# Talking-heads attention and gated network: rows issued ahead of stores, and some loads issued by GpSimd instead of SyncE

## The chip, the cores and the metric

One core of one Trainium2 chip runs the kernel. The metric is the device time of one execution in microseconds, median of several; lower is better. The engines are TensorE (PE, with its weight loads as PEld), VectorE (DVE), ScalarE (ACT), GpSimd (POOL) and SyncE (SP). SP does no arithmetic: it only issues DMAs, in program order, and waits before an issue for what that DMA needs. POOL and ACT can issue DMAs too, each in its own program order.

## The reference

```python
# q, k, v: (4, 12, 448, 64); w_pre, w_post: (12, 12)
scores = q @ k.T / sqrt(64)                                # per batch and head
scores = einsum('bhij,hg->bgij', scores, w_pre)            # heads mixed before the softmax
attn = exp(scores - max) ; attn = attn / (sum + 1e-9)
attn = einsum('bhij,hg->bgij', attn, w_post)               # and after it
out = attn @ v
x = out.transpose(0, 2, 1, 3).reshape(1792, 768)
result = (sigmoid(x @ w_gate) * (x @ w_val)) @ w_out       # 768 -> 1536 -> 768
```

All is float32 on the outside; the gated network's weights come in as 8-byte numbers, of which the kernel makes float32 itself.

## The kernel before

The kernel has two parts that overlap a little: the attention, which ends near 350 us, and the gated network, which runs to the end.

**The attention** goes over four batches, each with four blocks of query rows (three of 120 rows, one of 88). A block's scores are computed head pair by head pair (`scores`, line 159), copied from PSUM into a staging tile `st` (`keep`, line 165), and from there cut into *units* of 20 query rows (six units a block, five in the last block of a batch, 92 in all). For a unit, `regroup` (lines 203, 205) issues two DMAs that move rows of `st` into a tile `T`, so that the heads of a row lie on partitions; there are four T buffers. Then come `premix` (PE, line 213: heads mixed), `rowmax` (DVE, 218), `expo` (ACT, 225), `norm` (POOL 230, then DVE's reciprocal 231), `scale` (POOL, 237: the high half `ph`), `p_lo` (DVE, 243: the low half `pl`), `postmix` (PE, 255), `mix` (ACT, 263), and per block `av` (PE, 282), which ACT copies into a tile `xt` (line 292; one buffer for nearly all blocks). `xt` is put on a list `stores`, and `flush` issues its store to `xs` in DRAM (line 271, on SP).

The loop over *slots* s (line 404) sets the order. In a slot, in program order: `flush()`, the rows for unit s+6 (`rows_until(s + LEAD, ...)`, line 406), norm and scale of unit s+1, premix and rowmax of unit s+3, a score job, the first exp of unit s+3, p_lo of unit s+1, postmix and mix of unit s, the second exp of s+3, then what the plan has for this slot (loads of k, q and v among it), a piece of the gated network's work (`moe.slot`), and last `av` and the steps of `moe.early`. A block's `xt` are written at the ends of two slots two apart, and flushed at the start of the next slot.

The plan (lines 302 to 348) puts loads of a batch's `k` (six, line 137), a block's `q` (line 145) and a batch's `v` (three, line 172) into slots well ahead of their use, and the steps of eight weight tiles of the gated network (`early`, line 1032): four DMAs that load a tile in pieces into `raws` (line 1037), then steps on ACT, DVE and POOL that make float32 of it, and a DMA from POOL that keeps the result (line 1096). Before the change all of these loads are issued by SP, between the rows and the stores. The first batch's loads stand ahead of the loop and name their queue.

**The gated network** (class `_Moe`) multiplies in seven products per pair of tiles, on operands split into two float16 halves; PE's matmuls are on lines 1147 and 1158. A planner written in Python (`order_tasks`) fixes the order of its tasks.

Of the kernel before, what the change touches and what calls it, by code (L numbers as in the profile page):

```python
# [15 lines left out]
I8 = mybir.dt.int8  # L16
# [25 lines left out]
def _attention(ctx, tc, ins, B, H, S, D, xs, raws, make_moe):  # L42

    nc = tc.nc
    qp, kp, vb = (ins[n] for n in ("qp", "kp", "vb"))
    NQ = H // QUAD
    NP = H // 2
# [32 lines left out]
    def qk_banks():  # L80
        return [ps_qk.tile([128, 512], F32, tag="qk", name="qk") for _ in range(2)]
# [52 lines left out]

    def k_load(b, c, eng=None):
        t = kst.tile([128, S], F32, tag="k", name="k")
        (eng or nc.sync).dma_start(out=t, in_=kp[b, c])
        k_t[b, c] = t

    def q_load(bi, eng=None):  # L140

        b, i0, _, _, sets = blocks[bi]
        n = R * sets
        t = qst.tile([128, NP * QB], F32, tag="q", name="q")
        (eng or nc.sync).dma_start(out=t[:, :NP * n], in_=qp[b, :, NP * i0:NP * (i0 + n)])
        if n < 100:
            nc.gpsimd.memset(t[:, NP * n:NP * n + 100 - n], 0.0)
        q_t[bi] = [t[:, c * n:] for c in range(NP)]
# [4 lines left out]
    def scores(bi, c, sc):  # L153
        b, n = blocks[bi][0], R * blocks[bi][4]
        q, k = q_t[bi], k_t[b, c]
        for s0, s1 in ((0, 64), (64, max(n, 100))):
            for e in range(2):
                rows = slice(64 * e, 64 * e + 64)
                nc.tensor.matmul(sc[e][s0:s1, :S], lhsT=q[c][rows, s0:s1], rhs=k[rows, :], start=True, stop=True)  # L159

    def keep(bi, c, e, sc):
        n = R * blocks[bi][4]
        if c == e == 0:
            st_t[bi] = stg[bi % ST].tile([QB, H, S], F32, tag="st", name="st")
        (nc.vector.tensor_copy if e else nc.scalar.copy)(st_t[bi][:n, 2 * c + e], sc[e][:n, :S])  # L165
# [3 lines left out]

    def v_load(b, u):  # L170
        t = vst.tile([128, QUAD, 4, D], F32, tag="v", name="v")
        nc.sync.dma_start(out=t.rearrange("p h j d -> p (h j d)"), in_=vb[b, u])
        vt[b, u] = t


# [21 lines left out]
    def regroup(u):  # L197
        bi, r0s, _, _, i = units[u]
        sets, st, T = blocks[bi][4], st_t[bi], t_bufs[u % len(t_bufs)]
        at = 64 - HK  # L200
        for x in range(2):
            if len(r0s) == 2:
                nc.sync.dma_start(out=T[at:at + 2 * HK, x], in_=st[i + x:sets * R:sets])
            else:
                nc.sync.dma_start(out=T[at:at + HK, x], in_=st[i + sets * HALF * x:sets * HALF * (x + 1):sets])

    def premix(u):
        T = t_bufs[u % len(t_bufs)]
        banks = units[u][2]
        for x in range(2):  # L210
            for i, bank in enumerate(banks):
                rows = slice(64, 64 + HK) if i else slice(0, 64)
                nc.tensor.matmul(pm[bank][64 * x:64 * x + 64, :S], lhsT=w1[rows], rhs=T[rows, x], start=True, stop=True)  # L213

    def rowmax(u):
        nm = sm.tile([128, 2], F32, tag="nm", name="nm")
        for i, bank in enumerate(units[u][2]):
            nc.vector.tensor_reduce(nm[:, i:i + 1], pm[bank][:, :S], axis=AX.X, op=ALU.max, negate=True)  # L218
        nm_t[u] = nm

    def expo(u, i):
        if i == 0:
            e_t[u] = ep.tile([128, 2, S], F32, tag="e", name="e")
            ss_t[u] = sm.tile([128, 2], F32, tag="ss", name="ss")
        nc.scalar.activation(out=e_t[u][:, i], in_=pm[units[u][2][i]][:, :S], func=AF.Exp, bias=nm_t[u][:, i:i + 1],  # L225
                             scale=1.0, accum_out=ss_t[u][:, i:i + 1])

    def norm(u):
        ss = ss_t[u][:, :len(units[u][1])]
        nc.gpsimd.tensor_scalar(ss, ss, 1e-9, 1.0 / P_UP, op0=ALU.add, op1=ALU.mult)  # L230
        nc.vector.reciprocal(ss, ss)  # L231

    def scale(u):

        ph = pp.tile([128, 2, S], F16, tag="ph", name="ph")
        for i in range(len(units[u][1])):
            nc.gpsimd.tensor_scalar(ph[:, i], e_t[u][:, i], ss_t[u][:, i:i + 1], 1.0, op0=ALU.mult, op1=ALU.mult)  # L237
        p_t[u] = [ph]

    def p_lo(u):  # L240
        pl = pp.tile([128, 2, S], F16, tag="pl", name="pl")
        for i in range(len(units[u][1])):
            nc.vector.scalar_tensor_tensor(pl[:, i], e_t[u][:, i], ss_t[u][:, i:i + 1], p_t[u][0][:, i],  # L243
                                           op0=ALU.mult, op1=ALU.subtract)
        p_t[u].append(pl)
# [14 lines left out]
    def mix(u):  # L260
        bi, r0s = units[u][:2]
        out = mixes[bi % 2].rearrange("p j h s -> p (j h) s")[:, :, r0s[0]:r0s[-1] + R]
        nc.scalar.activation(out=out.rearrange("p g (y r) -> p y g r", r=HALF), in_=mx_t.pop(u), func=AF.Copy,  # L263
                             scale=1.0 / (P_UP * W_UP))
# [4 lines left out]
    def flush():  # L269
        while stores:  # L270
            nc.sync.dma_start(out=stores[0][0], in_=stores.pop(0)[1])
# [26 lines left out]
    LEAD = 6  # L298
# [12 lines left out]
    for b in range(B):  # L311
# [3 lines left out]
        s = f + 5  # L315
        for i in range(H // 2):
            s = max(s + 1, f + 6 + 2 * (2 * i // QUAD))
# [51 lines left out]
    for c in range(1, NP):  # L369
        k_load(0, c, nc.sync)  # L370
# [26 lines left out]
    def rows_until(u, done):  # L397
        while done < min(NU, u + 1):
            regroup(done)
            done += 1  # L400
        return done

    next_dma = 0
    for s in range(min(min(plan), -LEAD), max(plan) + 1):
        flush()
        next_dma = rows_until(s + LEAD, next_dma)
        todo = plan.get(s, ())
        jobs = [args for fn, args in todo if fn is scores]
        ahead_u = [(s + SOFT, i) for i in range(len(units[s + SOFT][1]))] if 0 <= s + SOFT < NU else []
        if 0 <= s + 1 < NU:  # L410
            norm(s + 1)
            scale(s + 1)
        if ahead_u:
            premix(s + SOFT)
            rowmax(s + SOFT)

        def job(bi, c):
            sc = qk_banks()
            scores(bi, c, sc)
            return lambda e: keep(bi, c, e, sc)  # L420

        kept = job(*jobs[0]) if jobs else None
        for i, e in enumerate(ahead_u[:1]):
            expo(*e)
        if kept:
            kept(0)
            kept(1)
        for c in hooks.get(s, ()):
            c.close()
        if 0 <= s + 1 < NU:  # L430
            p_lo(s + 1)
        tail = (av, moe.between, moe.early)
        if s == NU - 1:
            nc.scalar.activation(out=iw, in_=sw, func=AF.Sigmoid)
        if 0 <= s < NU:
            postmix(s)
        elif s >= NU:
            moe.slot(NG + s - NU)
        if 0 <= s < NU:
            mix(s)  # L440
        for e in ahead_u[1:]:
            expo(*e)
        for fn, args in todo:
            if fn is not scores and fn not in tail:
                fn(*args)
        if s >= NU - LEAD - 3:
            next_dma = rows_until(s + 1 + LEAD, next_dma)
        if 0 <= s < NU:
            for i in range(len(units[s][1])):
                moe.slot(units[s][3] + i)  # L450
        for fn, args in todo:
            if fn in tail:
                fn(*args)
        for args in jobs[1:]:
            kept = job(*args)
            kept(0)
            kept(1)
# [22 lines left out]
class _Moe:  # L480
# [14 lines left out]
    NP = 7  # L495
# [536 lines left out]
    def early(self, k, step):  # L1032

        raw = self.free["R"][k % len(self.free["R"])]
        if step < 4:
            b, e = 2 * self.WE * step, min(2 * self.WE * (step + 1), 8 * self.WE - 3)
            self.nc.sync.dma_start(out=raw.bitcast(I8)[:, b:e], in_=self.src[k].bitcast(I8)[:, b + 3:e + 3])
            return
        names = ("raw", k), ("half", k)
        self.at.update({names[0]: raw, names[1]: self.free["H"][0]})  # L1040
        if step < 9:
            self.top(k, (0, 0, 1, 2, 2)[step - 4], self.nc.vector if step > 5 else None, (0, 1, None, 0, 1)[step - 4])
        elif step < 11:
            self.convert(names[0], k, step - 9)
        elif step < 13:
            self.sum_of(names[0], ("w", k // 4), k % 4, step - 11, self.at[names[1]].bitcast(F16))
        else:
            self.keep_w(names[0], k)
        for name in names:
            del self.at[name]  # L1050
# [242 lines left out]
```

## Time and profile before

| what | value |
|---|---|
| median of 3 runs (lowest, highest) | 790.5 us (789.5, 790.78) |
| profiled execution: its own time | 792.71 us |
| profiled execution: span from first to last instruction | 790.9 us |
| PE busy | 765.7 us (97%) |
| DVE busy | 631.6 us (80%) |
| ACT busy | 566.5 us (72%) |
| POOL busy | 256.0 us (32%) |
| mean granted clock | 0.995 |
| HBM read, written | 87.77 MB, 38.15 MB |

The busy time of PE is modelled, so that a PE that is "busy" need not be at its peak. "Idle before" is the time in which an engine waited, with what ended the wait; where a wait is for several things, the one that came last by the profile is named, and where the engine named had long been done it was another. The chain that ended last is followed back from the last instruction to whatever released it. DMA issues that SP makes appear in the timeline as SPq; their duration is that of the issue and not of the transfer.

### The profile page before, as it was taken

How to read it: one execution, taken by the hardware profiler on the slowest of the kernel's cores; microseconds unless marked ns; L12 is line 12 of the kernel's file. 1: busy time of each engine (PE TensorE's matmuls, PEld its weight loads, DVE VectorE, ACT ScalarE, POOL GpSimd, SP SyncE). 2: the span in 40 equal slices, each digit the busy share in tenths (PEclk: the TensorE clock that was granted, in tenths of full speed). 3: DMA queues.
4: the chain of work that ended last, by engine and by line, in shares of the span. 5: the costliest groups of instructions: out<-in, count | busy, mean ns of one | idle time of the engine just before them, and what ended most of it. 6: DMA issues, size and time to landing. Idle time of an engine off the chain costs nothing.

```text
span 790.9 us, 23630 instructions
## 1 busy us (share of the span) xinstructions
PE 765.7 (97%) x9626; PEld 422.9 (53%) x9626; DVE 631.6 (80%) x1092; ACT 566.5 (72%) x1122; POOL 256.0 (32%) x426
## 2 busy tenths in 40 slices
PE   8999999899989999978999999999999999999998
PEld 2465665566656666554555455555555555555554
DVE  4998899699969898889996988679786999997111
ACT  3899899798989899786975877677856784563000
POOL 1563547354644455420312222224322221010000
PEclk9999999999999999999999999999999999999999
DMA  5787678747885474828506384664567788995001
GB/s 193 248 241 222 205 247 259 241 165 234 269 257 186 172 239 158 279 82 283 183 6 221 107 271 159 264 221 148 208 190 264 275 310 298 386 363 206 36 36 70
DMA packets 80716, 166.16 MB, mean 210 GB/s; under 512 B 20448, under 2 KB 57664, under 8 KB 80608
## 3 DMA queue, kind: packets, MB, share of 16 engines
q1 hardware_dynamic: 72304, 132.88, 50.8%
q0 software_dynamic: 7728, 31.27, 10.2%
q8 instruction: 75, 1.23, 0.6%
q10 hardware_dynamic: 576, 0.51, 0.2%
q14 instruction: 33, 0.27, 0.1%
HBM read 87.77 MB, written 38.15 MB: 159 GB/s over the span
## 4 chain that ended last, share of the span: by engine, by line
PE 83%; DVE 6%; ACT 5%; DMA 3%; issue 2%; POOL 1%; SPq 0%; DVEq 0%; ACTq 0%; POOLq 0%
PE bank L1147 30%; PE bank L1158 18%; PE pm L213 10%; PE qk L159 9%; PE av L282 8%; PE mx L255 7%; DVE m L1131 2%; ACT e L225 1%; ACT m L1126 1%; ACT mix L263 1%; DVE pl L243 1%; DMA T<-st 1%; DVE m L1140 1%; DMA max_w<-junk 1%; DMA k<-in_kp_dram 1%
## 5 line engine op out<-in xcount | busy, mean ns | idle before, releaser
L1147 PEld LDWEIGHTS <-m 128*128 128x128 f16 x1512 | 147.5, 98 | 143.3 <-DVE m L1131 4.1
L1147 PE MATMUL bank<-m,m 128*128 128x448 f16 x1116 | 214.7, 352 | 4.3 <-DVE m L1131 3.2
L237 POOL TENSOR_SCALAR ph<-e,ss 128x448 f16<-128x448 f32 x180 | 112.6, 638 | 151.6 <-DVE ss L231 108.7
L225 ACT ACTIVATE e<-pm,nm 128x448 f32<-128x448 f32 x180 | 115.4, 641 | 30.6 <-DVE nm L218 28.2
L218 DVE TENSOR_REDUCE nm<-pm 128x1 f32<-128x448 f32 x180 | 103.4, 615 | 31.7 <-PE pm L213 28.4
L243 DVE SCALAR_TENSOR_TENSOR pl<-e,ss,ph 128x448 f16<-128x448 f32 x180 | 115.8, 683 | 2.0 <-POOL ph L237 2.0
L213 PE MATMUL pm<-T,w 64*64 64x448 f32 (+1 forms) x720 | 109.7, 563 | 4.1 <-ACT raws L1078 3.5
L1158 PEld LDWEIGHTS <-m 128*128 128x128 f16 x756 | 74.0, 98 | 69.0
L159 PE MATMUL qk<-k,q 64*64 64x448 f32 x736 | 103.4, 545 | 2.8 <-ACT st L165 2.0
L263 ACT ACTIVATE mix<-mx 128x960 f32<-128x960 f32 (+1 forms) x92 | 104.5, 1136 | 1.4 <-PE mx L255 1.4
L255 PEld LDWEIGHTS <-ph 64*128 64x128 f16 x2880 | 63.4, 93 | 71.7 <-issue 42.3
L1158 PE MATMUL bank<-m,m 128*128 128x448 f16 x468 | 92.9, 352 | 0.0
L282 PE MATMUL av<-mix,v 128*64 128x120 f32 (+1 forms) x1504 | 83.8, 264 | 0.2 <-issue 0.2
L255 PE MATMUL mx<-w2hi,ph 64*128 64x60 f16 x1440 | 71.1, 189 | 7.6 <-ACT mix L263 5.2
L1147 PE MATMUL bank<-m 128*128 128x448 f16 x396 | 77.9, 352 | 0.0
L282 PEld LDWEIGHTS av<-mix,v 128*64 128x64 f32 x1504 | 73.6, 138 | 3.0 <-issue 0.8
L255 PE MATMUL mx<-w2lo,ph 64*128 64x60 f16 x1440 | 70.3, 188 | 1.0 <-issue 1.0
L255 PE MATMUL mx<-w2hi,pl 64*128 64x60 f16 x1440 | 70.1, 188 | 0.5 <-DVE pl L243 0.5
L1084 POOL CAST raws<-raws 128x768 f16<-128x768 bf16 x28 | 31.4, 1122 | 118.1 <-ACT raws L1078 118.1
L1078 ACT ACTIVATE raws<-raws 128x768 int16<-128x768 int8 (+1 forms) x72 | 60.2, 836 | 11.3 <-POOL raws L1084 11.1
L165 DVE COPY st<-qk 120x448 f32<-120x448 f32 (+1 forms) x92 | 56.6, 615 | 8.7 <-PE qk L159 8.7
L255 PEld LDWEIGHTS <-pl 64*128 64x128 f16 x1440 | 61.3, 93 | 1.7 <-issue 1.1
(127 smaller groups left out, 1043.1 us busy)
## 6 DMA issues: line engine op xcount, KB each, us to landing
T<-st SPq DMA_DIRECT2D x176, 210.0 KB
m<-w SPq DMA_DIRECT2D x60, 384.0 KB
raws<-in_w_dram SPq DMA_DIRECT2D x28, 767.6 KB
hs<-m POOLq DMA_DIRECT2D x48, 224.0 KB, 3.1
m<-hs SPq DMA_DIRECT2D x15, 672.0 KB
w<-m POOLq DMA_DIRECT2D x21, 384.0 KB, 4.4
w<-raws POOLq DMA_DIRECT2D x20, 384.0 KB, 4.7
v<-in_vb_dram SPq DMA_DIRECT2D x12, 512.0 KB
```

What stands on the lines that cost most here:

```text
L159: nc.tensor.matmul(sc[e][s0:s1, :S], lhsT=q[c][rows, s0:s1], rhs=k[rows, :], start=True, stop=True)
L213: nc.tensor.matmul(pm[bank][64 * x:64 * x + 64, :S], lhsT=w1[rows], rhs=T[rows, x], start=True, stop=True)
L218: nc.vector.tensor_reduce(nm[:, i:i + 1], pm[bank][:, :S], axis=AX.X, op=ALU.max, negate=True)
L225: nc.scalar.activation(out=e_t[u][:, i], in_=pm[units[u][2][i]][:, :S], func=AF.Exp, bias=nm_t[u][:, i:i + 1], scale=1.0, accum_out=ss_t[u ...
L237: nc.gpsimd.tensor_scalar(ph[:, i], e_t[u][:, i], ss_t[u][:, i:i + 1], 1.0, op0=ALU.mult, op1=ALU.mult)
L243: nc.vector.scalar_tensor_tensor(pl[:, i], e_t[u][:, i], ss_t[u][:, i:i + 1], p_t[u][0][:, i], op0=ALU.mult, op1=ALU.subtract)
L255: nc.tensor.matmul(mx[:, x, i, jb * HK:(jb + 1) * HK], lhsT=p[rows, i, JB[jb]:JB[jb] + 128], rhs=w[rows], start=(k == 0), stop=(k == 2))
L263: nc.scalar.activation(out=out.rearrange("p g (y r) -> p y g r", r=HALF), in_=mx_t.pop(u), func=AF.Copy, scale=1.0 / (P_UP * W_UP))
L282: nc.tensor.matmul(av_t[bi][64 * i:64 * i + 64, c % 4, :n], lhsT=vt[b, u][:, h + i, jb, :], rhs=mixes[bi % 2][:, jb, 2 * c + i, :n], start ...
L1078: self.nc.scalar.activation(out=out, in_=src, func=AF.Copy, scale=by)
L1147: self.nc.tensor.matmul(self.f32(bank), lhsT=w[a][:, k], rhs=x[b][:, k], start=self.START[i] and k == r == 0, stop=k == self.KH - 1 and r ...
L1158: self.nc.tensor.matmul(self.f32(bank), lhsT=w[a][:, k], rhs=b[bb], start=self.START[i] and j == k == r == 0, stop=j == OUT_TILES - 1 and ...
```

## The change

In the slot loop the two first lines change places: the rows for unit s+6 are issued before the list of stores is flushed. And four kinds of loads are issued by GpSimd instead of SyncE: k, q and v inside the loop, and the four pieces of each early weight tile. The loads ahead of the loop that name their queue stay as they are, as do the gated network's other loads (`load_raw`, `load_w`, `load_x` and others on SP). Sizes, tiles and the plan's slots don't change.

```diff
     def k_load(b, c, eng=None):
         t = kst.tile([128, S], F32, tag="k", name="k")
-        (eng or nc.sync).dma_start(out=t, in_=kp[b, c])
+        (eng or nc.gpsimd).dma_start(out=t, in_=kp[b, c])
...
     def q_load(bi, eng=None):
...
-        (eng or nc.sync).dma_start(out=t[:, :NP * n], in_=qp[b, :, NP * i0:NP * (i0 + n)])
+        (eng or nc.gpsimd).dma_start(out=t[:, :NP * n], in_=qp[b, :, NP * i0:NP * (i0 + n)])
...
     def v_load(b, u):
         t = vst.tile([128, QUAD, 4, D], F32, tag="v", name="v")
-        nc.sync.dma_start(out=t.rearrange("p h j d -> p (h j d)"), in_=vb[b, u])
+        nc.gpsimd.dma_start(out=t.rearrange("p h j d -> p (h j d)"), in_=vb[b, u])
...
     for s in range(min(min(plan), -LEAD), max(plan) + 1):
+        next_dma = rows_until(s + LEAD, next_dma)
         flush()
-        next_dma = rows_until(s + LEAD, next_dma)
         todo = plan.get(s, ())
...
     def early(self, k, step):
...
-            self.nc.sync.dma_start(out=raw.bitcast(I8)[:, b:e], in_=self.src[k].bitcast(I8)[:, b + 3:e + 3])
+            self.nc.gpsimd.dma_start(out=raw.bitcast(I8)[:, b:e], in_=self.src[k].bitcast(I8)[:, b + 3:e + 3])
```

## Rows read from the trace of the kernel before

**Rows 1.** The page, part 4: the chain that ended last, by engine.

```profile
PE 83%; DVE 6%; ACT 5%; DMA 3%; issue 2%; POOL 1%; SPq 0%; DVEq 0%; ACTq 0%; POOLq 0%
```

**Rows 2.** Busy us by stretch: PE, PEld, DVE, ACT, POOL, granted clock, DMA share, GB/s.

```profile
120.00:160.00 40.00, 36.74 (x808) 21.92 (x808) 32.52 (x71) 34.41 (x83) 19.69 (x30) 1.00 0.76 240
...
200.00:240.00 40.00, 37.99 (x815) 22.38 (x811) 32.94 (x74) 34.69 (x82) 21.20 (x31) 0.96 0.84 259
240.00:280.00 40.00, 40.00 (x948) 25.22 (x942) 35.97 (x79) 36.17 (x87) 18.99 (x38) 1.00 0.53 180
...
400.00:440.00 40.00, 40.00 (x214) 20.70 (x212) 32.08 (x45) 27.23 (x48) 9.28 (x13) 1.00 0.41 142
440.00:480.00 40.00, 39.01 (x206) 19.99 (x205) 36.50 (x65) 31.25 (x60) 10.03 (x13) 1.00 0.55 188
```

**Rows 3.** Timeline of PE, premixes: start us, us, operation [idle before <-releaser].

```profile
127.82 1.22 PE L213 MATMUL pm<-T,w 64*64 64x448 f32 x8
...
145.78 1.24 PE L213 MATMUL pm<-T,w 64*64 64x448 f32 x5 [2.40 <-ACT raws L1078]
...
154.74 0.98 PE L213 MATMUL pm<-T,w 64*64 64x448 f32 x8
...
209.65 0.98 PE L213 MATMUL pm<-T,w 64*64 64x448 f32 x8
...
238.91 0.98 PE L213 MATMUL pm<-T,w 64*64 64x448 f32 x8
```

**Rows 4.** Row-max instructions alone by stretch: DVE, ACT, clock, DMA share, GB/s.

```profile
155.00:211.00 56.00, 17.89 (x32) 23.46 (x64) 1.00 0.69 215
```

**Rows 5.** Busy us by short stretch, columns as in Rows 2.

```profile
226.00:228.00 2.00, 0.58 (x30) 0.35 (x22) 1.86 (x4) 0.40 (x2) 0.00 (x0) 1.00 0.67 236
...
230.00:232.00 2.00, 2.00 (x13) 0.67 (x6) 0.56 (x2) 1.73 (x5) 0.57 (x2) 0.50 0.66 233
```

**Rows 6.** Timeline of ACT, writes of xt.

```profile
133.40 0.66 ACT L292 ACTIVATE xt<-av,sw 128x480 f32<-128x480 f32 x1
...
144.79 0.46 ACT L292 ACTIVATE xt<-av,sw 128x240 f32<-128x240 f32 x1 [3.56 <-DMA xs<-xt]
...
227.60 0.46 ACT L292 ACTIVATE xt<-av,sw 128x240 f32<-128x240 f32 x1 [1.79 <-PE mx L255]
```

**Rows 7.** The chain that ended last, in order of time: start us, us, what.

```profile
221.52 6.46 DMA T<-st
```

**Rows 8.** Timeline of SP: start us, us for the issues, line, DMA.

```profile
137.09 0.38 SPq L271 DMA_DIRECT2D xs<-xt  x1
137.65 1.67 SPq L203 DMA_DIRECT2D T<-st  x2
...
219.71 0.38 SPq L271 DMA_DIRECT2D xs<-xt  x1
220.62 1.67 SPq L203 DMA_DIRECT2D T<-st  x2
```

**Rows 9.** SP's waits, 0 to 322 us: who <- for whom: us, times, longest.

```profile
SPq L271 <- ACT xt L292: 53.6, 24, 5.4
```

**Rows 10.** POOL by line: duration in ns, shortest, median, longest.

```profile
L1096 POOL DMA_DIRECT2D w<-raws x20: 539/552/736, 87.0 to 586.8; - x20
...
L230 POOL TENSOR_SCALAR ss<-ss x92: 181/192/2055, 20.5 to 341.7; 128x2 f32<-128x2 f32 x88, 128x1 f32<-128x1 f32 x4
```

**Rows 11.** Timeline of POOL.

```profile
86.96 0.74 POOL L1096 DMA_DIRECT2D w<-raws  x1
87.78 0.64 POOL L230 TENSOR_SCALAR ss<-ss 128x2 f32<-128x2 f32 x1
88.79 1.25 POOL L237 TENSOR_SCALAR ph<-e,ss 128x448 f16<-128x448 f32 x2 [0.37 <-PE av L282]
...
388.88 1.73 POOL L1112 DMA_DIRECT2D hs<-m  x3 [0.68 <-DVE m L1180]
```

**Rows 12.** DVE's waits, 20 to 320 us: who <- for whom: us, times, longest.

```profile
DVE nm L218 <- PE pm L213: 25.8, 33, 2.5
```

## The prediction

> **What bounds the kernel now.** I read the chain that ended last first: TensorE (PE) holds 83% of it, transfers 3%, GpSimd (POOL) 1% [rows 1]. So time is to be had only where PE stands still or crawls. The stretches of 40 us show where: from 400 us on, in the gated network, PE is busy all the time or all but 1 us in 40, and so it is at 240 to 280 us in the attention; 120 to 160 and 200 to 240 us are short by 3.3 and 2.0 us of PE time, and in the second the granted clock is 0.96 [rows 2]. Both lie in the attention, where the change works.
>
> The attention is a loop of 92 units, and PE's start on a unit's premix (line 213) marks its pace. From 154.74 to 209.65 us it does 16 units [rows 3, 4] (two row-max reductions a unit, 32 of them): 54.91 / 16 = 3.43 us a unit. From 127.82 to 154.74 it does six in 26.92 us, where 6 x 3.43 = 20.6 were due: 6.3 us lost. From 209.65 to 238.91 it does seven in 29.26 us against 24.0: 5.2 us lost. Together 11.5 us.
>
> What stood in the way, first stretch: ACT waits 3.56 us before it writes xt at 144.79, for the store that still reads the one xt buffer [rows 6]. That xt had been written by 133.40 + 0.66 = 134.06, but SP issued its store only at 137.09 [rows 8], 3.0 us late, and it read the buffer until 144.79: 7.7 us. PE meanwhile waits 2.40 us for the premix at 145.78 [rows 3]; the row names a raw-weight step of ACT, which a premix doesn't need. It needs T rows, issued at 137.65 behind that store [rows 8], and a PSUM bank that the held-up ACT reads: I take both to be late. Second stretch: the chain holds one transfer of T from 221.52 for 6.46 us [rows 7]; those rows were issued at 220.62, again just behind a store of 219.71 [rows 8], and ACT stood 1.79 us before its next xt at 227.60 [rows 6]. PE is busy 0.58 of 2 us at 226 to 228, and at 230 to 232 the granted clock is 0.50, the 1.2 GHz level [rows 5]. That is within the 5.2 us.
>
> So the losses are late T rows and late stores, on one queue with the loads, in the two stretches in which k, v, q and raw pieces for the next batch are loaded together. SP also waits 53.6 us in total, 24 times, for an xt before a store [rows 9], with T rows behind it.
>
> **The change part by part.**
>
> Rows before stores. No instruction is added. In slot s the rows of unit s+6 need a T buffer that the premix of unit s+2 gave back in slot s-1, and staged scores; the store needs an xt of the end of slot s-1. So rows rarely wait longer than the store, and no longer sit behind the 53.6 us, 2.2 us a time. The store now has a pair of row issues ahead of it: 1.67 us [rows 8]. Cost of that: two xt writes of a block are two slots apart, 6.9 us at 3.43, so a store that leaves 1.7 us after its xt has about 5 us before it holds ACT; it costs nothing unless the transfer takes longer than that, and up to 1.7 us each time if it does.
>
> Loads moved. In the loop's plan I count 18 loads of k, 14 of q, 12 of v and 32 raw pieces: 76 DMAs leave SP and go to POOL, all in slots -4 to 75, none near the end; the prologue names its queues itself. What it removes: SP issues T rows and stores without them in between, and neither stands behind the loads' packets in one queue. All of the 11.5 us goes if T and stores are in time. What it leaves: the same bytes in the same slots, on the same transfer engines. Store waits left over: nothing at best; all of 3.56 + 1.79 = 5.35 us at worst. If the travel stayed 7.7 us and only the issue came earlier (at most 1.7 us after the xt instead of 3.0), 2.3 of the 3.56 us stay. I take 1.5 us for both together, nearer to nothing, since a store no longer follows k, q and raw packets in its queue. T rows I take as hidden: a buffer comes back at the premix of unit u-4, four units or 13.7 us before it is needed, of which issue takes 1.7 and the worst travel shown 6.46 (T) to 7.7 (the store).
>
> POOL pays. A DMA issue there takes 0.54 to 0.74 us [rows 10]; three in a row took 1.73, so 0.57 each [rows 11]. That is 43 to 56 us of POOL over 76. A unit costs POOL 1.25 for the scaled pair, 0.19 (median) and a gap of 0.09 for the norm, 0.37 until the reciprocal is back [rows 10, 11]: 1.9 us. With n DMAs at 0.57: n = 2 gives 3.04, within 3.43; n = 4 gives 4.18, 0.75 over. Five slots (6, 8, 29, 31, 52) have four, one (54) has three and 0.2 over: 3.9 us if all of it lands on the path. At 0.74 it is 1.4 x 5 + 0.7 = 7.8 us. At the low end nothing: DVE waits 25.8 us for premixes between 20 and 320 us [rows 12], right after the reciprocal that POOL would hold up, so a late norm eats that idle time first. I take 1.5 us, 0.5 in each of three bursts, near the cheap row, because a burst's first issue falls beside DVE's pl, where POOL's next norm is held anyway (0.64 us in the row behind an issue of 0.74 [rows 11], up to 2055 ns against a median of 192 [rows 10]).
>
> POOL is in order, so a DMA that waits would hold norm and scale of the next unit, then DVE's reciprocal and pl, then PE's postmix. I see no data wait: q's old buffer was last read three slots earlier, k's a batch earlier, v's two slots earlier; the raw pieces' buffer was copied out ten slots earlier. What could wait is an issue for an earlier transfer of the same queue to land; no row of POOL's shows one in the attention, where it has only eight DMAs, one for each tile kept.
>
> The Trainium skill ("DMA: Bandwidth & Descriptors", SWDGE vs HWDGE vs iDMA) has a rule that speaks against this change: GpSimd writes its DMA descriptors into SBUF, which DVE can lock it out of, while DMAs issued by SP are immune. The trace agrees in kind, with the 0.74 beside the 0.54; by the rule the dear end, 7.8 us, would hold and the sum would be -2.2, so 788.
>
> **The sum**, against the profiled execution: span 790.9 us in a time of 792.71, so 1.8 outside. -11.5 + 1.5 (stores) + 1.5 (POOL) = -8.5: span 782.4, time 784.2. From 400 us on PE is busy throughout, so what starts 8.5 us earlier ends 8.5 us earlier. That execution is 2.2 us above the median of the runs, 790.5; from the median: **782.0**.
>
> **Rivals.**
> 1. The bytes stay in the way. T and stores are as slow as now because the transfer engines are as full (0.76 and 0.84 in the two stretches [rows 2]); only earlier issue helps. Then 1.3 us of the first wait goes, and of the second stretch all but ACT's 1.79: 1.3 + 3.4 = 4.7, less POOL's 1.5: 787.3. For it: the store took 7.7 us with loads ahead of it. Against: those were in its own queue. By the Trainium skill (the same page, Issuing engines are not separate DMA queues), spreading DMAs over engines saves only issue time; that is this rival, and no row settles it.
> 2. POOL becomes the bound, and the kernel is slower. Slots 6 to 9, 29 to 32 and 52 to 55 have 12, 12 and 11 DMAs on POOL then, kept tiles included, in 4 x 3.43 = 13.7 us. POOL's own work takes 4 x 1.9 = 7.6, leaving 6.1: 0.51 us a DMA. At 0.57 the overflow is 0.7 a burst; at 0.74 it is 2.8, 8.3 in all, and the gain is nearly spent. It decides from 0.83 us each, where 3 x 3.8 = 11.5; at 1.0 us (issues held by earlier ones, or by DVE) it is 3 x 5.9 - 11.5 = 6 us slower: 797. Against: no issue above 0.74 among the 20 on that line.
> 3. The next thing is late at once. ACT and DVE are nearly full in the attention, and the lost time is only handed on: 790.
> 4. Nothing is paid and units elsewhere gain too: 777.
>
> **How the numbers follow.** Forecast (779 to 785.5) 0.56; rival 1 (785.5 to 789) 0.18; rival 2 (over 792) 0.12; rival 3 0.09; rival 4 0.05. What a measurement can tell from no change is about 0.2%, 1.6 us. Faster: 0.56 + 0.18 + 0.05 = 0.79; same 0.09; slower 0.12. The bounds reach from -11.5 (779) to -11.5 + 5.35 + 7.8 = +1.65 (792). The range 777.5 to 791 leaves out rival 2 and part of rival 4, about 0.16.
>
> **What would show it.** After: the units that took 26.92 and 29.26 us at 3.4 to 3.6 us each; no transfer of T of several us on the chain; ACT's xt wait for a store at most 1 us; no stretch at half clock there; T rows issued a slot earlier. POOL's DMA issues at 0.55 to 0.75. Wrong if ACT or PE waits for stores or T as now (rival 1), if DVE's reciprocal or pl waits for POOL in the four-DMA slots (rival 2), or if a unit still takes over 4 us in those stretches while DVE and ACT have no idle time (rival 3).

## The result, and the profile after

The changed kernel takes **798.1 us** (median of six runs, 795.4 to 802.0) against 791.1 us for the kernel before beside it (789.5 to 793.1): ratio 1.0093, 95% interval 1.0070 to 1.0116. It is slower by some 7 us; 782.0 had been forecast. Its profiled execution has a span of 796.4 us in a time of 798.2.

The chain that ended last, the rows of after that answer to [rows 1]:

```profile
PE 74%; DMA 7%; DVE 7%; ACT 7%; issue 2%; POOL 2%; SPq 0%; ACTq 0%; DVEq 0%; POOLq 0%
```

PE has lost 9 points of the chain, and transfers have 7% in place of 3%. The same chain in order of time (start us, us, what) says which; these are its longest transfers in the attention:

```profile
55.18 9.12 DMA xs<-xt
...
130.94 13.89 DMA T<-st
...
222.66 9.23 DMA xs<-xt
```

Two stores of x and one transfer of T rows, in the kernel before one transfer of T of 6.46 us [rows 7]. ACT's waits for a store (who <- for whom: us, times, longest):

```profile
ACT xt L292 <- DMA xs<-xt: 8.3, 3, 3.6
```

The writes of xt behind them, in ACT's timeline, against waits of 3.56 and 1.79 us in [rows 6]:

```profile
64.39 0.46 ACT L292 ACTIVATE xt<-av,sw 128x240 f32<-128x240 f32 x1 [2.75 <-DMA xs<-xt]
...
148.64 0.46 ACT L292 ACTIVATE xt<-av,sw 128x240 f32<-128x240 f32 x1 [3.63 <-DMA xs<-xt]
149.00 0.53 ACT L1078 ACTIVATE raws<-raws 128x384 int16<-128x384 int8 x1
149.43 0.62 ACT L225 ACTIVATE e<-pm,nm 128x448 f32<-128x448 f32 x1
149.95 0.20 ACT L225 ACTIVATION_READ_ACCUMULATOR e<-pm,nm 128x1 f32 x1
...
231.97 0.46 ACT L292 ACTIVATE xt<-av,sw 128x240 f32<-128x240 f32 x1 [1.91 <-DMA xs<-xt]
```

The second wait is as long as before, the third too, and the first is new. SP's timeline has the stores that caused the last two, with the rows around them (compare [rows 8]):

```profile
125.23 9.11 SPq L203 DMA_DIRECT2D T<-st  x8
...
138.03 0.37 SPq L271 DMA_DIRECT2D xs<-xt  x1
138.49 6.30 SPq L203 DMA_DIRECT2D T<-st  x4
...
222.66 0.37 SPq L271 DMA_DIRECT2D xs<-xt  x1
223.13 3.01 SPq L203 DMA_DIRECT2D T<-st  x3
```

PE's premixes at the ends of the two stretches (34 to 40 and 56 to 63 of the units), and a stop within the first:

```profile
131.48 0.96 PE L213 MATMUL pm<-T,w 64*64 64x448 f32 x5
...
150.20 0.60 PE L213 MATMUL pm<-T,w 60*64 60x448 f32 x3 [1.93 <-ACT e L225]
...
158.61 0.98 PE L213 MATMUL pm<-T,w 64*64 64x448 f32 x8
...
213.51 0.98 PE L213 MATMUL pm<-T,w 64*64 64x448 f32 x8
...
241.48 0.98 PE L213 MATMUL pm<-T,w 64*64 64x448 f32 x8
```

Six units take 158.61 - 131.48 = 27.13 us (26.92 before [rows 3]); seven take 27.97 (29.26 before). So of the 11.5 us that should have gone, 1.1 went. The stop at 150.20 shows the path: ACT waits for the store until 148.64, casts a raw piece, reads the bank until 149.95 + 0.20 = 150.15, and only then may PE write that bank.

By stretch of 40 us, columns and stretches as in [rows 2], with 320 to 360 added:

```profile
120.00:160.00 40.00, 36.78 (x802) 20.96 (x794) 31.37 (x66) 33.82 (x81) 24.97 (x47) 1.00 0.78 247
200.00:240.00 40.00, 37.57 (x825) 21.95 (x824) 34.37 (x79) 36.10 (x86) 25.88 (x49) 1.00 0.81 258
240.00:280.00 40.00, 40.00 (x936) 24.68 (x932) 35.79 (x77) 35.93 (x84) 21.11 (x42) 1.00 0.56 187
320.00:360.00 40.00, 33.22 (x705) 24.22 (x704) 31.77 (x50) 31.28 (x56) 11.68 (x22) 0.87 0.51 163
400.00:440.00 40.00, 40.00 (x213) 20.64 (x211) 31.11 (x38) 26.45 (x45) 8.45 (x12) 1.00 0.31 106
440.00:480.00 40.00, 37.78 (x199) 19.28 (x198) 37.02 (x67) 30.82 (x59) 10.56 (x14) 1.00 0.55 193
```

The time of the same PE instruction in both traces gives the ledger of after less before: +0.5 us by 50 us, +2.7 by 66 (the new wait), +3.7 by 124, +3.9 at 200 (the first stretch gains nothing), +2.6 by 245 (the second gains), +3.8 by 365 (the granted clock is 0.87 at 320 to 360), +5.2 by 455 and to the end (PE 37.78 us busy at 440 to 480, where before had 39.01). The last step is scatter: over the profiled executions below it lies anywhere from -1.3 to +1.4 us, and no edit reaches there. The step of 1 us at 340 to 365 stands in eight of the eleven other traces that can be laid beside before so; the cause isn't settled. So of the 5.5 us between these two executions the attention holds 2.8 up to 340 us; what ties the slower median to the new waits is the run with a second xt buffer below.

POOL, whose price was one of the two in doubt, from 0 to 340 us (line, operation, count | busy us, mean ns | idle before):

```profile
L230 POOL TENSOR_SCALAR ss<-ss 128x2 f32<-128x2 f32 (+1 forms) x90 | 30.5, 338 | 19.3 <-ACT e L225 12.2
L1037 POOL DMA_DIRECT2D raws<-in_w_dram x32 | 18.1, 565 | 0.0
L137 POOL DMA_DIRECT2D k<-in_kp_dram x18 | 10.4, 577 | 0.0
L145 POOL DMA_DIRECT2D q<-in_qp_dram x14 | 8.0, 568 | 7.7 <-PE qk L159 7.7
L172 POOL DMA_DIRECT2D v<-in_vb_dram x12 | 7.0, 584 | 0.0
```

32 + 18 + 14 + 12 = 76 issues, 43.5 us, 0.57 us each: the count and the cheap row of the prediction.

### The profile page after: what moved, and what is told of

Read it like the earlier page. It is cut to its first block, busy times and chain, and to the rows that moved or that the text cites. A ratio compares the mean times of both kernels' runs of the same rounds, so it can differ in the third digit from the quotient of the medians.

```text
span 796.4 us, 23651 instructions
## 1 busy us (share of the span) xinstructions
PE 768.5 (96%) x9626; PEld 423.5 (53%) x9626; DVE 631.7 (79%) x1092; ACT 566.6 (71%) x1122; POOL 281.7 (35%) x502
## 3 DMA queue, kind: packets, MB, share of 16 engines
q0 software_dynamic: 13776, 52.78, 19.3%
## 4 chain that ended last, share of the span: by engine, by line
PE 74%; DMA 7%; DVE 7%; ACT 7%; issue 2%; POOL 2%; SPq 0%; ACTq 0%; DVEq 0%; POOLq 0%
PE bank L1147 31%; PE bank L1158 18%; PE pm L213 7%; PE av L282 7%; PE qk L159 6%; PE mx L255 5%; DMA xs<-xt 3%; DMA T<-st 2%; ACT e L225 2%; DVE pl L243 2%; DVE nm L218 1%; ACT mix L263 1%; DVE m L1131 1%; DMA max_w<-junk 1%; POOL ph L237 1%
## 5 line engine op out<-in xcount | busy, mean ns | idle before, releaser
L159 PE MATMUL qk<-k,q 64*64 64x448 f32 (+1 forms) x736 | 101.5, 541 | 3.4 <-ACT st L165 3.0
L1174 DVE TENSOR_TENSOR m<-bank,m 128x448 f32<-128x448 f32 x72 | 44.3, 618 | 22.3 <-PE bank L1147 14.1
```

## The experiments

Travel below is from a store's issue to its landing, by the trace's completion counts (the same number as the chain's row where the chain has one, 9.12 at 55 us). Each ratio is that of a kernel's runs to those of the kernel before in the same group (not always the quotient of the medians), with its 95% interval.

**Each part alone.** Rows ahead of stores, loads left on SP:

```diff
-        flush()
         next_dma = rows_until(s + LEAD, next_dma)
+        flush()
```

> The kernel before with the rows put ahead of the stores and all loads left on SP. Theory A (stores lose in their turn): once the loads have a queue of their own, each of a store's 480-byte packets waits behind a packet of several KB of GpSimd's queue, so stores travel 9 to 10.5 us where they took 6 to 7.8, and ACT waits for the xt buffer; here the loads share SP's queue again, so stores travel 6 to 8 us in the three bursts, ACT waits 2 to 5 us in all, and T rows are early: 784 to 789 us. Theory B (GpSimd pays: its 76 issues delay norm and scale): no issue is moved here, so 784 to 789 as well. Theory C (rows ahead of stores make the stores late): about 797, with stores of 9 us.

Measured: 796.9 us, 1.0061 (1.0037 to 1.0084). Loads on POOL, stores first:

```diff
-        (eng or nc.sync).dma_start(out=t, in_=kp[b, c])
+        (eng or nc.gpsimd).dma_start(out=t, in_=kp[b, c])
...
```

> The kernel before with the loads moved to GpSimd and the stores still ahead of the rows. Theory A: as slow as the change, 795 to 800 us, stores travel about 9 us in the bursts, ACT waits for xt about 8 us in all. Theory B: the same 795 to 800, but with DVE or PE waiting for GpSimd and not ACT for the store. Theory C: 783 to 788, stores of 6 us or less.

Measured: 793.7 us, 1.0032 (1.0011 to 1.0053). The first time is Theory C's, without its stores of 9 us; the second lies in none of the three ranges. Each part is slower by itself, and 0.61 + 0.32 add up to the 0.93% of both (each known to about 0.2). The three stores took 6.8, 6.8 and 7.7 us with rows first (issued up to 2.7 us after xt was ready), 6.9, 9.3 and 7.7 with loads moved, 9.1, 10.5 and 9.2 with both, against 6.0, 7.6 and 7.8 before. ACT's waits for them sum to 5.0 and 2.7 us.

**The store's small packets.** The changed kernel with x stored in long rows; x is laid out another way there, so later steps read other elements of it:

```diff
...
+            if b < B - 1:
+                to = xs[b, c0:c + 1].rearrange("c p s -> (c p s)").rearrange("(p r) -> p r", p=128)[:, m * i0:m * (i0 + n)]
...
```

> The changed kernel with the stores of the first three batches written as rows of 1920 bytes (four chunks side by side for each partition) instead of four of 480: the same bytes, a quarter of the packets, in an order in which the gated network would not find its x (it reads other elements, same sizes). Theory A: a quarter of the turns to wait for, so stores travel 4 to 6 us in the bursts instead of 9 to 10.5 and ACT hardly waits: 785 to 790 us. Theory B and Theory C: stores travel as long as in the changed kernel, 795 to 799. A theory D, that the transfer engines are simply full of bytes: stores as long as in the changed kernel, 795 to 799.

Measured: 795.9 us, 1.0060 (1.0039 to 1.0081). The stores took 9.4, 11.0 and 12.2 us: long rows, behind T rows in SP's queue, don't land sooner. So Theory A's 4 to 6 us falls; whether long rows would land sooner in a queue of their own no run shows.

**The place in SP's queue.** The changed kernel with stores of x on ACT's queue:

```diff
-            nc.sync.dma_start(out=stores[0][0], in_=stores.pop(0)[1])
+            nc.scalar.dma_start(out=stores[0][0], in_=stores.pop(0)[1])
```

> The changed kernel with one line more: the stores of x leave from ACT's queue, which carries no other transfer in this stage, so no T row and no load stands ahead of a store. A store then costs ACT about 0.4 us of issue (24 of them before 320 us, some 10 us of ACT time, most of it beside its waits for row maxima), so the total is no clean comparison and the travel times decide. Theory C (order in SP's queue makes the stores late): the three stores that took 9.1, 10.5 and 9.2 us land within 6 us of their issue, and ACT's waits for xt fall from 8.3 to under 2 us; time 787 to 795. Theory D (the sixteen transfer engines are full there, whoever is first): the three still take 8 us or more, and the waits stay at 6 to 9 us; time 797 to 803.

Measured: 808.9 us, 1.0219 (1.0186 to 1.0252). From ACT's timeline, store and next xt:

```profile
142.18 0.37 ACTq L271 DMA_DIRECT2D xs<-xt  x1
...
153.67 0.46 ACT L292 ACTIVATE xt<-av,sw 128x240 f32<-128x240 f32 x1 [4.23 <-DMA xs<-xt]
```

With nothing ahead of it in its queue the store still takes 11.4 us here, 11.8 at 55 and 10.7 at 231 us. To stand first in its queue doesn't make it land sooner. (The total is above both ranges; it also holds ACT's own issues, so it prices nothing.)

**What the moved loads do to T rows and stores.** The traces show it in the DMA queues (packets, MB, share of 16 engines; q1 is SP's, q0 GpSimd's), 130 to 145 us, in the kernel before:

```profile
q1 hardware_dynamic: 2563, 3.59, 79.2%
q0 software_dynamic: 80, 0.39, 6.4%
```

And in the changed kernel:

```profile
q0 software_dynamic: 827, 3.02, 64.9%
q1 hardware_dynamic: 937, 1.25, 28.7%
```

Before, one queue carries nearly all, and what SP issues there lands in the order of issue. After, the packets of the two queues are about as many, but GpSimd's are nearly three times as large, and SP's queue, which holds only T rows and stores there, moves 1.25 of 4.3 MB. So the loads overtake: one of k that GpSimd issued at 139.18 landed at 145.76, T rows that SP issued at 132.72 at 147.10. The longest T transfer of units 36 to 40 took 7.4 to 8.3 us in the five traces with the loads on SP (before and rows first, with and without the buffer below, rows first twice), 9.8 to 15.5 in the four with the loads on GpSimd (loads moved alone: 15.5); the three stores took 4.0 to 7.8 against 6.8 to 10.5. In the run with stores on ACT's queue (q10), 145 to 152 us:

```profile
q0 software_dynamic: 323, 1.26, 47.2%
q1 hardware_dynamic: 337, 0.56, 21.8%
q10 hardware_dynamic: 436, 0.21, 10.2%
```

Again the packets are of like number, and the store, in packets of 480 bytes, moves the fewest bytes. So a queue of its own doesn't help it. That the engines take a packet of each queue in turn would fit these counts; no run shows the turns themselves. Fuller the engines were not: while the store of units 34 to 40 travelled they moved 284 GB/s before and 278 after.

**The single xt buffer.** A block's second xt gets a buffer of its own, paid for by a scratch tile of one byte an element:

```diff
-    v_abs = const.tile([128, 2 * 4 * D], BF16, name="v_abs")
+    v_abs = const.tile([128, 2 * 4 * D], I8, name="v_abs")
...
-                xt = xp.tile([128, 4, QB], F32, tag="xt", name="xt")[:, :c + 1 - c0, :n]
+                xt = xp.tile([128, 2 if c0 else 4, QB], F32, tag=f"xt{c0}", name="xt")[:, :c + 1 - c0, :n]
```

In the changed kernel:

> The changed kernel with a buffer of its own for a block's second xt (and the scratch of the v sums in 8 bits, to make room), so that no xt is written over one still being stored. Theory A: ACT's waits for xs<-xt (8.3 us) go, stores travel as long as in the changed kernel: 784 to 789 us. Theory B: 795 to 799. Theory C: as A, 784 to 789, since the late store then holds nobody.

Measured: 788.7 us, 0.9953 (0.9929 to 0.9977). In the kernel before, in rows first and in loads moved:

> The kernel before with a buffer of its own for a block's second xt and nothing of the change. If the single xt buffer was the whole loss in the two stretches, ACT's waits of 3.56 and 1.79 us go and the time falls by about 5 us, to 784 to 787, below the 788.7 of the changed kernel with the same buffer. If late T rows are the next thing behind it, as the prediction has it, the waits go over into waits for T and the time falls by 0 to 2.5 us, to 788.5 to 791, so that the change is worth something once the buffer is there.

> Rows ahead of stores alone, with the second xt buffer. If the 5 us that this part lost by itself came from stores landing late, they are gone with the buffer and the earlier T rows show: 784 to 788, under the same kernel with stores first by 1 to 3 us. If this part also loses in another way (PE stood still for 1.53 and 1.76 us at 201 and 209 us with no releaser in the trace), the time stays 2 us or more above the one with stores first.

> Loads from GpSimd's queue alone, with the second xt buffer. If the loads that GpSimd issues cost only through late stores, the time falls from 793.7 to 785 to 788. If they cost through GpSimd's own time (some 76 issues of 0.55 us beside its two 0.62 us operations per unit), the time stays above 790.

Measured: before with the buffer 790.0, 0.9965 (0.9940 to 0.9989); rows first 787.0, 0.9950 (0.9927 to 0.9973); loads moved 790.0, 0.9991 (0.9970 to 1.0012). Loads moved lies at the edge of the range for a cost of GpSimd's own time, but no higher than the kernel before with the buffer, so no such cost can be told. With the buffer the change costs nothing that these runs can tell (788.7 beside 790.0); without it, it costs 0.93%. Time between premixes, one trace each, tells why (us; due at 3.43 a unit: 17.2, 20.6, 24.0):

| kernel | units 12 to 17 | 34 to 40 | 56 to 63 |
|---|---|---|---|
| before | 17.9 | 26.9 | 29.3 |
| rows first | 20.2 | 25.8 | 25.8 |
| loads moved | 18.6 | 26.3 | 27.0 |
| both (the change) | 20.7 | 27.1 | 28.0 |
| before, own buffer | 17.8 | 26.7 | 27.7 |
| rows first, own buffer | 17.9 | 23.1 | 27.4 |
| loads moved, own buffer | 18.3 | 25.1 | 26.6 |
| both, own buffer | 17.9 | 23.8 | 25.9 |

A second trace of rows first (below) has 19.3, 25.4 and 30.3 here, so the last column can't be read to less than 4.5 us. In units 34 to 40 earlier rows alone gain 1.1 us, the buffer alone 0.2, and both 3.9. (The trace of the buffer alone has a granted clock of 0.89 at 135 to 150 us, where the others of the square have 1.00, so its 0.2 is a low figure.) Two things ended together there in the kernel before: T rows landed at 145.65 and 146.39 (two transfers), and the held-up ACT had read the bank at 146.30:

```profile
146.10 0.20 ACT L225 ACTIVATION_READ_ACCUMULATOR e<-pm,nm 128x1 f32 x1
```

The premix lines of before with the buffer, where ACT waits for no store any more:

```profile
145.57 1.89 PE L213 MATMUL pm<-T,w 64*64 64x448 f32 x6 [2.54 <-ACT e L225]
...
230.16 1.08 PE L213 MATMUL pm<-T,w 64*64 64x448 f32 x6 [1.53 <-DMA T<-st]
```

The first names ACT, but the first of its T transfers landed at 145.43, so it is that which ended the wait; the second names them. In units 12 to 17 the buffer takes the change's whole 2.8 us back. Before had no wait there only by a hair, as ACT's timeline of the kernel before shows:

```profile
60.39 0.68 ACT L178 ACTIVATE v_abs<-v 128x512 bf16<-128x512 f32 x1
60.91 0.26 ACT L178 ACTIVATION_READ_ACCUMULATOR v_abs<-v 128x1 f32 x1
61.00 0.51 ACT L292 ACTIVATE xt<-av,sw 128x240 f32<-128x240 f32 x1
```

The store of 54.71 landed at 60.75, 0.25 us before ACT came to 61.00; no view of waits shows it. (In the trace of before with the buffer that store took 4.0 us instead of 6.0, so the room is that of one execution.) In the changed kernel that store takes 9.12 us.

**How full the transfer engines are.** The six loads of the next batch's k went out over about four slots. Spread over 20 (third and fourth batch) or 9 (second), same bytes and queues:

```diff
-            at(spread(c, NP, first[PB * (b - 1)] + 6, first[PB * b - 1] - LEAD - 2), k_load, b, c)
+            at(spread(c, NP, max(1, first[PB * (b - 1)] - 10), first[PB * b - 1] - LEAD - 2), k_load, b, c)
```

> The changed kernel with the same bytes in the same queues, only the six loads of the next batch's k (224 KB each) issued over 20 slots instead of 4 for the third and fourth batch, and over 9 instead of 4 for the second, where the trace had a full stretch each time. Theory D (a stretch in which the transfers together ask for what the engines can move, about 270 GB/s, makes every store late, whatever its place): the stores that took 10.5 and 9.2 us land within 6 us, the waits of ACT for xt at 148 and 232 us go (5.5 of 8.3 us), the first, at 64 us, shrinks in part; time 789 to 793. If it is rather the order in SP's queue or GpSimd's queue as such, the travel stays at 9 us or more and the time at 796 to 799.

> The kernel before with the same spread of the k loads and nothing of the change. Theory D: the two stretches that lost 6.3 and 5.2 us shrink to 2 us or less each, and the time falls by 6 to 11 us, to 780 to 785, without the change. If the loss came from the order of stores and rows in SP's queue, as the prediction has it, k's transfers there count little and the time stays within 2 us of before, 789 to 793.

> The changed kernel with the spread k loads and a buffer of its own for a block's second xt. If the engines' full stretches and the single xt buffer are together the whole loss, this gives 779 to 784; if the change has costs of its own (GpSimd's issues, or PE's stops without a releaser), it stays at 786 to 789, no better than with the buffer alone.

Measured: the changed kernel 793.7, 1.0041 (1.0012 to 1.0069); the kernel before 791.8, 1.0015 (0.9995 to 1.0035); the changed kernel with the buffer 792.7, 1.0025 (1.0003 to 1.0047). SP's timeline of the first, the store in the stretch of units 34 to 40:

```profile
137.43 0.37 SPq L271 DMA_DIRECT2D xs<-xt  x1
137.90 2.73 SPq L203 DMA_DIRECT2D T<-st  x3
```

ACT's timeline of it, the xt that waited 3.63 us in the changed kernel:

```profile
144.22 0.51 ACT L292 ACTIVATE xt<-av,sw 128x240 f32<-128x240 f32 x1
144.57 0.61 ACT L1078 ACTIVATE raws<-raws 128x384 int16<-128x384 int8 x1
```

Busy us by stretch, columns as in [rows 2], of the changed kernel:

```profile
135.00:150.00 15.00, 12.78 (x246) 6.61 (x242) 10.54 (x22) 11.37 (x29) 10.09 (x19) 1.00 0.82 272
```

And of it with the spread loads:

```profile
135.00:150.00 15.00, 15.00 (x328) 8.73 (x324) 13.09 (x27) 15.00 (x38) 8.67 (x17) 1.00 0.75 243
```

The store took 6.7 us instead of 10.5, ACT doesn't wait, PE is busy all 15 us instead of 12.78, and the engines move 243 GB/s there instead of 272. The later one took 4.9 instead of 9.2. The two stretches took 23.4 and 25.9 us (27.1 and 28.0), in the kernel before 23.6 and 26.4 (26.9 and 29.3). So with fewer loads in the stretch the stores land sooner in the changed kernel, and the stretches shorten in either queue order, if not quite as far as Theory D gave (6 us, 789 to 793). As a remedy it failed: the totals expected for the kernel before and for the one with the buffer were some 7 and 9 us too low, and 791.8 lies in the range of the other account. The kernel before with spread loads is already 2.2 us behind by 50 us and 3.7 by 66, where the second batch's loads now go out at 29 to 55 us beside T rows of the first batch; why the total with the buffer got worse is only argued from that.

**A second trace of rows first.** In the first one PE stood still twice with no releaser in the trace:

```profile
202.85 0.60 PE L213 MATMUL pm<-T,w 60*64 60x448 f32 x3 [1.53 <-issue]
...
210.49 0.20 PE L255 MATMUL mx<-w2hi,ph 64*128 64x60 f16 x2 [1.76 <-issue]
```

> Rows ahead of stores alone once more, for a second trace: if PE's two stops at 201 and 209 us, of 1.53 and 1.76 us with no releaser in the trace, belong to this order, they stand there again within 0.3 us; if they are scatter of one execution, that stretch (units 40 to 56) takes 55 us as in the kernel before instead of 60.4.

Measured: 796.0 us in one run. Units 40 to 56 took 56.4 us instead of 60.4, and neither stop is there; instead units 56 to 63 took 30.3 (25.8), with a wait of 3.77 us for a store. So the stops don't belong to a place in this order. What they are stays open: they begin in the midst of a group of matmuls that waits for nothing, and eight of the other thirteen traces, before's too, have one of about 1 us or more in the attention (0.96 in before's).

## Why the prediction was wrong

**What bounds the kernel: right about where, half right about what.** Two of the three stretches were found, and the loss there is of late stores and late T rows. But it was read as one queue's order, to be freed step by step. In the first stretch it is two limits that ended together, each able to hold it alone; in the second, one trace of each kernel can't tell.

**Rows before stores, "costs nothing unless the transfer takes longer than that": it did.** This sentence held the price, and I let it stand at nothing with a 7.7 us travel already in the rows. Alone, rows first issued two of the three stores 1.8 and 2.7 us after their xt (1.7 had been the bound), and ACT waited 5.0 us. In the whole change they left at once but took 9 to 10.5 us. The wait at 144.79 became one at 148.64, 3.56 against 3.63: the store was issued 3 us sooner after its xt and took 3 us longer.

**"Store waits left over: 1.5 us", nearer to nothing "since a store no longer follows k, q and raw packets in its queue": this term failed.** They were 8.3 us, above the upper bound of 5.35, which counted only waits that before already had. The reason failed with it, the wrong way round: loads in a queue of their own overtook T rows and stores, which stood in one line with them before. Moved alone, they made the store of 7.6 us one of 9.3. And in a queue of its own a store took 11 us.

**"T rows I take as hidden", worst travel 6.46 to 7.7: failed.** They were issued earlier, as forecast, and the chain shows 13.89 us for one. For unit 38 (premix at 145.78 before, 147.30 after) they were issued 8 us before it, then 14.6, and the first of the two transfers landed 0.14 us before it, then 0.20. The longer travel goes with the moved loads and not with the earlier issue: the longest T transfer of units 36 to 40 took 8.3 us before, 7.4 with rows first alone, 15.5 with loads moved alone, where no rows go ahead. With the buffer as well the chain's longest T there is 8.48 us, and that unit's first transfer lands 4.9 us ahead. So -11.5 came to -1.1 in the two stretches, and to -6.5 with the buffer, one trace each: the mechanism exists, behind another.

**POOL, 1.5 us: no cost shows.** The issues took 0.57 us and the norm's mean is 338 ns, where the trace of before has 505; with the buffer the kernel takes 790.0 us with the loads on either engine. Rival 2, the one that gave a slower kernel, named the wrong engine; that its 797 is near is luck.

**Rival 1 came nearest** (the bytes stay in the way, the engines as full), but gave it 787.3, since it priced the travel as fixed and earlier issue as pure gain. What it held against itself, that the loads had been in the store's own queue, is what had kept the travel short.

**Not seen at all:** the stretch of units 12 to 17. It lost 0.7 us before, so nothing was looked at, and it lost 2.8 more after. The slower side lay in a wait that did not exist yet, not in one to be shortened.

## What to carry to other kernels

Before loads are moved to another queue, look at what the transfer engines carry there and what else has to land: where they moved 265 to 275 GB/s, transfers of one queue landed in the order of issue, and loads in a second queue, in larger packets, overtook the rows and stores that were needed first. Look for the waits that almost happen: take each buffer's landing against the moment its next writer arrives, and where there is 0.25 us of room with a single buffer, buy the second buffer first. When two limits end together, test them as a square of four kernels; one at a time they gave 1.1 and 0.2 of the 3.9 us.

The fastest kernels here are rows first with the second buffer (787.0 us) and the whole change with it (788.7); the runs don't tell these two apart, and both beat the kernels before and after.

## What the runs showed of the hardware

A store of 240 KB that took 2.4 us where the engines moved 153 GB/s (245 and 265 us of the kernel before) took 4.0 to 7.8 in full stretches behind loads of its own queue, 6.8 to 10.5 with the loads in GpSimd's, 10.7 to 11.8 alone in ACT's, and 9.4 to 12.2 in long rows. Of queues that worked side by side the engines moved packets in like number (827 and 937; 323, 337 and 436), so that the one with larger packets moved more bytes (3.02 MB to 1.25; 1.26 to 0.56 and 0.21). By the Trainium skill ("DMA: Bandwidth & Descriptors", Issuing engines are not separate DMA queues), spreading DMAs over engines saves only issue time; the trace agrees so far that the moved loads made nothing land sooner, and differs in that it was no saving: 0.32% slower alone. Of the rule that DVE can lock GpSimd out of its descriptors (the same page, SWDGE vs HWDGE vs iDMA) 76 issues of 565 to 584 ns on average show no sign.
